# The output projection turned channel-major, with its store in 128-byte pieces and image blocks placed through DRAM

## The chip, the cores and the metric

The kernel runs on one core of a Trainium2 chip. The metric is the device time of one execution in microseconds (us), as a median over runs. The engines are TensorE (PE in the profile; its weight loads are PEld), VectorE (DVE), ScalarE (ACT), GpSimd (POOL) and SyncE (SP; here it only issues DMAs, and its queue appears as SPq).

## The reference, cut to what matters

```python
# attention with keys and values pooled 4x4 from an image, then a gated feed-forward
kv_pool = kv.reshape(B, H // r, r, W // r, r, C).mean(axis=(2, 4))     # r = 4
k = v = kv_pool.reshape(B, -1, C) @ w_sr                               # 768 keys per image
x = softmax((q @ k.T) / sqrt(C)) @ v                                   # 4 x 12288 tokens, C = 128
out = (np.maximum(x @ w_gate, 0.0) * (x @ w_val)) @ w_out              # d_ff = 1536
```

The kernel cuts the 49,152 tokens into 96 tiles of 512 (T) and the hidden layer into 12 blocks of 128 (NFB). Four tiles are a group (GRP); there are 24 groups.

## The kernel before

All stages are spread over one software pipeline: in iteration k, tile k is scored, tile k-1 takes its values, tile k-3 goes through the gated layer, and tile k-4 through the output projection. Each iteration has 12 steps, one per hidden block. The output projection uses the hidden block as the stationary operand, so four products of 128 columns are needed for 512 tokens, and the result has tokens on the partitions, ready to be stored in 2 KB rows:

```python
    def out_add(k, fb, s, o_ps, first):
        nc.tensor.matmul(
            o_ps, hTs[k][:, fb, s * 128 : (s + 1) * 128], wo16[:, fb, :],
            start=first, stop=(fb == NFB - 1), skip_group_check=True,
        )

    def out_proj(k, fb):
        if fb == 0:
            o_banks[k] = bank([128, NS, 128])
        for s in range(NS):
            out_add(k, fb, s, o_banks[k][:, s, :], fb == 0 and s == 0)

    def out_scale(k, engine, own, o_ps=None):
        if k not in o_sbs:
            o_sbs[k] = work.tile([128, NS, 128], FP32, tag="o_sb", bufs=3, name="o_sb")
        o_sb, o_ps = o_sbs[k][:, own], o_ps if o_ps is not None else o_banks[k]
        if engine is nc.scalar:
            nc.scalar.mul(o_sb, o_ps, 1.0 / X_SCALE**2)
        else:
            nc.vector.tensor_scalar(o_sb, o_ps, 1.0 / X_SCALE**2, None, op0=ALU.mult)

    def out_store(k, own):
        nc.sync.dma_start(
            out[k // GRP * GRP * T : (k // GRP + 1) * GRP * T, :].rearrange(
                "(p i s) c -> i p s c", p=128, i=GRP
            )[k % GRP][:, own], o_sbs[k][:, own],
        )
        if own.stop == NS:
            for tiles in (hTs, o_banks, o_sbs):
                del tiles[k]
```

Image blocks for the next image are turned while this one is computed: VectorE transposes within 32 by 32 blocks, and sixteen small DMAs put the blocks in their places (the iterations with this work are called image stages below, the others plain stages):

```python
    def turn_blocks(b, pair):

        blocks = work.tile([128, 2, C], FP32, tag="kv_blocks", bufs=2)
        nc.vector.transpose(
            blocks.rearrange("p h c -> p (h c)"), s3s.pop((b, pair)).rearrange("p h c -> p (h c)")
        )
        kv_Ts[b, pair] = work.tile([128, 2, 128], FP32, tag="kvT", bufs=2, name="kvT")
        return [(kv_Ts[b, pair], blocks, i, j) for i in range(4) for j in range(4)]

    def block_move(kvT, blocks, i, j):
        rows, columns = slice(32 * i, 32 * (i + 1)), slice(32 * j, 32 * (j + 1))
        nc.sync.dma_start(kvT[columns, :, rows], blocks[rows, :, columns])
...
                    if not odd and 2 <= step < 10:      # in the main loop
                        for _ in range(2):
                            block_move(*moves.pop())
```

The transposed x, on which the gated layer waits, comes from a DMA transpose in the same queue of SyncE, issued at the last step of an iteration (`x_turn(k - 1)`).

The softmax here doesn't subtract the row's maximum and nothing guards it: scores larger than these inputs give would overflow.

## Time and profile before

| | before |
|---|---|
| median time, 3 runs | 1043.85 us (1042.52 to 1044.16) |
| TensorE busy | 99% of the span |
| time of one tile in the steady part | 10.52 us |
| VectorE, ScalarE busy within such a tile | 9.36 and 9.39 us |
| DMA engines, mean share | about 36% |

A high busy share of TensorE does not show what a product costs, because matmul records overlap. The distance from one start to the next does. A line of the groups view gives line, engine, operation, output and input tiles, shape and count; then busy us and mean ns of one; then the idle time just before and what ended it. A transfer's landing is its completion, counted from its issue. Here is one stretch of SyncE's queue in an image stage, from the timeline of the kernel before (start in us, length in us, line, operation, tiles, count):

```profile
212.04 11.41 SPq L202 DMA_DIRECT2D kvT<-blocks  x16
223.55 0.53 SPq L307 DMA_DIRECT2D out_dram<-o_sb  x1
224.19 1.27 SPq L251 DMA_TRANSPOSE xT<-x  x1
```

The sixteen block moves hold this in-order queue for 11.41 us, longer than a tile, and the x transpose stands behind them. At this place TensorE did not wait, at three others it did.

### The profile page before, as it was taken

The numbers are of one execution on the slowest core, as the hardware profiler recorded it, in microseconds if no ns is written. First come the engines' busy times: TensorE is split into PE (matmuls) and PEld (weight loads), VectorE is DVE, ScalarE is ACT, GpSimd is POOL, SyncE is SP. The second block draws the span as 40 slices with busy tenths as digits, with TensorE's granted clock in tenths as the row PEclk, the third lists the DMA queues.
The fourth block names the chain that finished last, engine by engine and source line by source line (L and its number), as shares of the span: only waits on it lengthen the run. The fifth ranks groups of instructions, "written<-read, shape, count | busy, mean of one in ns | idle before, by whom it ended". The sixth has DMA issues, their size and how long they took to land.

```text
span 1041.0 us, 26051 instructions
## 1 busy us (share of the span) xinstructions
PE 1032.3 (99%) x9924; PEld 684.2 (66%) x9924; DVE 911.7 (88%) x1668; ACT 909.8 (87%) x1750; POOL 106.6 (10%) x128
## 2 busy tenths in 40 slices
PE   8999999999999999999999999999999999999998
PEld 5666666666666666666666666666666666666665
DVE  3889888898888888988888888989888888888898
ACT  4988888888888888888888888888888888888887
POOL 2000045100000015400000003440000000000000
PEclk9999999999999999999999999999999999999999
DMA  8734254441322345533223134561431322212111
GB/s 304 136 65 87 91 164 128 95 88 41 87 61 58 72 132 148 145 71 82 65 52 88 31 88 133 158 151 42 91 82 37 78 62 52 67 31 67 32 47 47
DMA packets 140253, 92.53 MB, mean 89 GB/s; under 512 B 117728, under 2 KB 118624, under 8 KB 140128
## 3 DMA queue, kind: packets, MB, share of 16 engines
q1 hardware_dynamic: 134544, 77.56, 27.7%
q0 software_dynamic: 5440, 13.24, 7.7%
q8 instruction: 77, 1.26, 0.5%
q14 instruction: 48, 0.39, 0.1%
q10 hardware_dynamic: 144, 0.07, 0.0%
HBM read 52.76 MB, written 25.17 MB: 75 GB/s over the span
## 4 chain that ended last, share of the span: by engine, by line
PE 96%; DMA 3%; SPq 0%; ACT 0%; issue 0%; DVE 0%
PE bank_ps L286 25%; PE bank_ps L265 24%; PE bank_ps L276 24%; PE bank_ps L227 12%; PE bank_ps L216 11%; DMA parts<-in_kv_dram 1%; DMA q<-in_q_dram 1%; DMA xT<-x 1%; PE bank_ps L180 0%; SPq L131 0%; ACT aT L217 0%; PE bank_ps L154 0%; PE bank_ps L172 0%; SPq L93 0%; PE bank_ps L258 0%
## 5 line engine op out<-in xcount | busy, mean ns | idle before, releaser
L279 DVE SCALAR_TENSOR_TENSOR hT<-bank_ps,val 128x512 f16<-128x512 f32 x1152 | 760.6, 687 | 99.3 <-ACT val L269 74.2
L269 ACT CAST val<-bank_ps 128x512 f16<-128x512 f32 x1152 | 678.5, 591 | 111.5 <-PE bank_ps L265 109.8
L286 PEld LDWEIGHTS <-hT 128*128 128x128 f16 x4608 | 353.1, 98 | 203.6 <-issue 0.2
L286 PE MATMUL bank_ps<-wo,hT 128*128 128x128 f16 x4608 | 443.6, 219 | 0.0
L265 PE MATMUL bank_ps<-xT,wv 128*128 128x512 f16 x1152 | 436.6, 379 | 0.4 <-DMA xT<-x 0.2
L276 PE MATMUL bank_ps<-xT,wg 128*128 128x512 f16 x1152 | 436.6, 379 | 0.0
L217 ACT ACTIVATE aT<-bank_ps 128x512 f16<-128x512 f32 x576 | 346.2, 605 | 0.9 <-PE bank_ps L216 0.8
L227 PE MATMUL bank_ps<-kv,aT 128*128 128x129 f16 x2304 | 223.5, 220 | 0.5 <-DVE kv L189 0.4
L227 PEld LDWEIGHTS <-aT 128*128 128x128 f16 x2304 | 177.2, 98 | 68.3 <-issue 0.9
L216 PE MATMUL bank_ps<-qT,kv 128*128 128x512 f16 x576 | 216.8, 379 | 0.4 <-DVE qT L114 0.2
L276 PEld LDWEIGHTS <-wg 128*128 128x128 f16 x1152 | 112.7, 98 | 65.8 <-issue 0.2
L265 PEld LDWEIGHTS <-wv 128*128 128x128 f16 x1152 | 112.7, 98 | 1.4 <-DMA xT<-x 0.9
L243 DVE TENSOR_TENSOR x<-bank_ps,rinv 128x256 f16<-128x256 f32 x188 | 79.7, 425 | 6.7
L78 POOL DMA_DIRECT2D q<-in_q_dram x23 | 12.5, 544 | 550.2 <-DMA qT<-q 549.8
L304 DVE TENSOR_SCALAR o_sb<-bank_ps 128x512 f32<-128x512 f32 (+1 forms) x95 | 64.0, 674 | 1.3 <-PE bank_ps L286 1.3
L140 POOL TENSOR_TENSOR s<-parts 128x512 f32<-128x512 f32 x36 | 45.3, 1270 | 164.1 <-DMA parts<-in_kv_dram 161.2
L216 PEld LDWEIGHTS <-kv 128*128 128x128 f16 x576 | 56.1, 98 | 2.9 <-ACT kv L174 0.8
L235 DVE RECIPROCAL rinv<-bank_ps 128x2 f32<-128x2 f32 x192 | 30.7, 160 | 0.6 <-PE bank_ps L227 0.6
L142 POOL TENSOR_TENSOR s<-s 128x512 f32<-128x512 f32 x18 | 22.8, 1268 | 1.4
L144 POOL TENSOR_TENSOR c<-s 128x256 f32<-128x256 f32 x18 | 13.1, 727 | 1.4
L165 ACT COPY kvT<-bank_ps 128x128 f32<-128x128 f32 x4 | 1.1, 266 | 10.4 <-PE bank_ps L154 9.5
L167 DVE COPY kvT<-bank_ps 128x128 f32<-128x128 f32 x2 | 0.6, 292 | 10.0 <-PE bank_ps L154 10.0
(48 smaller groups left out, 78.3 us busy)
## 6 DMA issues: line engine op xcount, KB each, us to landing
parts<-in_kv_dram SPq DMA_DIRECT2D x48, 512.0 KB, 6.2
out_dram<-o_sb SPq DMA_DIRECT2D x95, 256.0 KB, 2.1
q<-in_q_dram POOLq DMA_DIRECT2D x23, 512.0 KB, 5.4
kvT<-blocks SPq DMA_DIRECT2D x144, 8.0 KB, 1.8
xT<-x SPq DMA_TRANSPOSE x94, 2.5
q<-in_q_dram SPq DMA_DIRECT2D x2, 512.0 KB, 7.9
wv<-in_moe_w_val_dram POOLq DMA_DIRECT2D x2, 192.0 KB, 4.4
wg<-in_moe_w_gate_dram POOLq DMA_DIRECT2D x2, 192.0 KB, 5.2
```

The source lines that it names most:

```text
L140: eng.tensor_tensor(s2[:, i], parts[:, 2 * i, h], parts[:, 2 * i + 1, h], op=ALU.add)
L216: nc.tensor.matmul(s_ps, kv16[:, k // NST, jc, 0:C], qT_of(k), start=True, stop=True)
L217: nc.scalar.activation(aTs[k][:, jc, :], s_ps, AF.Exp, scale=qk_scale)
L227: nc.tensor.matmul(x_ps[:, i, :], aTs[k][:, jc, s * 128 : (s + 1) * 128], kv16[:, k // NST, jc, C : 2 * C + 1], start=(jc == 0 and i == 0) ...
L235: nc.vector.reciprocal(rinvs[k, half], x_banks[k, half][:, :, C : C + 1])
L243: nc.vector.tensor_tensor(x16s[k][:, 2 * half : 2 * half + 2, :], x_ps[:, :, 0:C], rinv.to_broadcast([128, 2, C]), op=ALU.mult,)
L265: nc.tensor.matmul(va_ps, wv16[:, fb * 128 : (fb + 1) * 128], xTs[k], start=True, stop=True)
L269: nc.scalar.copy(val, va_ps)
L276: nc.tensor.matmul(g_ps, wg16[:, fb * 128 : (fb + 1) * 128], xTs[k], start=True, stop=True)
L279: nc.vector.scalar_tensor_tensor(hTs[k][:, fb, :], g_ps, 0.0, vals.pop((k, fb)), op0=ALU.max, op1=ALU.mult)
L286: nc.tensor.matmul(o_ps, hTs[k][:, fb, s * 128 : (s + 1) * 128], wo16[:, fb, :], start=first, stop=(fb == NFB - 1), skip_group_check=True,)
L304: nc.vector.tensor_scalar(o_sb, o_ps, 1.0 / X_SCALE**2, None, op0=ALU.mult)
```

## The change

The intent is to relieve TensorE: with the output weights stationary and the hidden block moving, one product of 512 columns does the work of four, and three of four weight loads go. The result then has channels on the partitions, so VectorE transposes it in 32 by 32 blocks and GpSimd scales and arranges it. Only 32 channels of a token stay together, so the store is in pieces of 128 B. To let one store cover 16 tokens of a partition, the q load orders the tokens differently, in four DMAs; the first and last group keep the old order and take 16 stores per tile. The image blocks are placed by one store to DRAM and four loads. The last two tiles keep the old output path.

```diff
         q16 = work.tile([128, GRP * NS, C], FP16, tag="q16", bufs=2)
-        nc.gpsimd.dma_start(
-            q16, q[b, n0 : n0 + GRP * T, :].rearrange("(p s) c -> p s c", p=128)
-        )
+        rows = q[b, n0 : n0 + GRP * T, :]
+        if g in (0, NG - 1):
+            nc.gpsimd.dma_start(q16, rows.rearrange("(p s) c -> p s c", p=128))
+        else:
+            rows = rows.rearrange("(i t j s) c -> j t i s c", i=GRP, t=32, s=NS)
+            for j in range(4):
+                nc.gpsimd.dma_start(
+                    q16[32 * j : 32 * (j + 1)].rearrange("t (i s) c -> t i s c", i=GRP), rows[j]
+                )
         q16s[g] = q16
 
     def q_turn(g):
...
-        blocks = work.tile([128, 2, C], FP32, tag="kv_blocks", bufs=2)
+        blocks = work.tile([128, 4, 2, 32], FP32, tag="kv_blocks", bufs=2)
         nc.vector.transpose(
-            blocks.rearrange("p h c -> p (h c)"), s3s.pop((b, pair)).rearrange("p h c -> p (h c)")
-        )
-        kv_Ts[b, pair] = work.tile([128, 2, 128], FP32, tag="kvT", bufs=2, name="kvT")
-        return [(kv_Ts[b, pair], blocks, i, j) for i in range(4) for j in range(4)]
-
-    def block_move(kvT, blocks, i, j):
-        rows, columns = slice(32 * i, 32 * (i + 1)), slice(32 * j, 32 * (j + 1))
-        nc.sync.dma_start(kvT[columns, :, rows], blocks[rows, :, columns])
+            blocks.rearrange("p j h c -> p (j h c)"),
+            s3s.pop((b, pair)).rearrange("p j h c -> p (j h c)"),
+        )
+        placed = dram.tile([128, 256], FP32, tag="blocks", bufs=2)
+        nc.sync.dma_start(placed, blocks.rearrange("p j h c -> p (j h c)"))
+        kvT = work.tile([128, 4, 2, 32], FP32, tag="kvT", bufs=2, name="kvT")
+        kv_Ts[b, pair] = kvT
+        rows = placed.rearrange("(i p) (j x) -> j p i x", p=32, j=4)
+        return [
+            (kvT[32 * j : 32 * (j + 1)].rearrange("p i h c -> p i (h c)"), rows[j])
+            for j in range(4)
+        ]
 
     def turn_values_dma(b, pair):
         for jc in (2 * pair, 2 * pair + 1):
...
     def out_proj(k, fb):
+        if k == NT - 2:
+            if fb == 0:
+                o_banks[k] = bank([128, NS, 128])
+            for s in range(NS):
+                out_add(k, fb, s, o_banks[k][:, s, :], fb == 0 and s == 0)
+            return
         if fb == 0:
-            o_banks[k] = bank([128, NS, 128])
-        for s in range(NS):
-            out_add(k, fb, s, o_banks[k][:, s, :], fb == 0 and s == 0)
+            o_banks[k] = bank([128, T])
+        nc.tensor.matmul(
+            o_banks[k], wo16[:, fb, :], hTs[k][:, fb, :], start=fb == 0, stop=fb == NFB - 1
+        )
+
+    def out_turn(k):
+
+
+        o_t = work.tile([128, T], FP32, tag="o_t", bufs=2)
+        nc.vector.transpose(o_t, o_banks.pop(k))
+        o_sb = work.tile([128, 4, NS, 32], FP32, tag="o_sb", bufs=3)
+        nc.gpsimd.tensor_scalar(
+            o_sb.rearrange("t j s c -> t s j c"),
+            o_t.rearrange("t (s j c) -> t s j c", s=NS, j=4),
+            1.0 / X_SCALE**2, None, op0=ALU.mult,
+        )
+        del hTs[k]
+        g = k // GRP
+        rows = out[g * GRP * T : (g + 1) * GRP * T, :]
+        moves = []
+        for b in range(4):
+            o_b = o_sb[32 * b : 32 * (b + 1)]
+            if g in (0, NG - 1):
+                to = rows.rearrange("(j t i s) (b c) -> b i j t s c", j=4, t=32, s=NS, c=32)
+                moves += [(to[b, k % GRP, j], o_b[:, j]) for j in range(4)]
+            else:
+                to = rows.rearrange("(i t r) (b c) -> b i t r c", t=32, r=16, c=32)
+                moves.append((to[b, k % GRP], o_b.rearrange("t j s c -> t (j s) c")))
+        return moves
 
...
                 if step == NFB - 1 and k < last:
-                    out_scale(kO, nc.vector if kF < NT - 2 else nc.scalar, slice(0, NS))
-                    out_store(kO, slice(0, NS))
+                    out_moves = out_turn(kO)
+            if 2 <= step < 10:
+                for _ in range(2):
+                    if out_moves:
+                        nc.sync.dma_start(*out_moves.pop())
...
-                    if not odd and 2 <= step < 10:
-                        for _ in range(2):
-                            block_move(*moves.pop())
+                    if moves and step > 4:
+                        nc.sync.dma_start(*moves.pop())
```

Left out are the layout of the pooled sums (four column blocks outermost, so that a block's pieces are contiguous), the matching layout in `project`, and one buffer fewer for a pooling intermediate.

More of the change, by code (lines that the diff above doesn't have):

```diff
@@ L64 @@
     work = ctx.enter_context(tc.tile_pool(name="work", bufs=2))
+    dram = ctx.enter_context(tc.tile_pool(name="dram", bufs=1, space=bass.MemoryType.DRAM))
     psum = ctx.enter_context(tc.tile_pool(name="psum", bufs=8, space=bass.MemoryType.PSUM))
@@ L137, in pool_pixels @@
         parts = kv_in[b, pair]
-        s2 = work.tile([128, 2, r, C], FP32, tag="kv_s2", bufs=3)
+        s2 = work.tile([128, 2, r, C], FP32, tag="kv_s2", bufs=2)
         for i in range(2):
@@ L145, in pool_pixels @@
         if h == 0:
-            s3s[b, pair] = work.tile([128, 2, C], FP32, tag="kv_s3", bufs=2, name="kv_s3")
-        eng.tensor_tensor(s3s[b, pair][:, h], c2[:, 0], c2[:, 1], op=ALU.add)
+            s3s[b, pair] = work.tile([128, 4, 2, 32], FP32, tag="kv_s3", bufs=2, name="kv_s3")
+        c4 = c2.rearrange("p i (j c) -> p i j c", c=32)
+        eng.tensor_tensor(s3s[b, pair][:, :, h], c4[:, 0], c4[:, 1], op=ALU.add)
     def turn_add(chunk, lines, first=False):
@@ L178, in project @@
     def project(b, pair):
-        pr = bank([128, 2, 128])
+        pr = bank([128, 4, 2, 32])
         nc.tensor.matmul(pr, w_sr_f32, kv_Ts.pop((b, pair)), start=True, stop=True)
         nc.vector.tensor_scalar(
-            kv16[:, b, 2 * pair : 2 * pair + 2, 0:C], pr, 1.0 / (r * r), None, op0=ALU.mult
+            kv16[:, b, 2 * pair : 2 * pair + 2, 0:C].rearrange("c h (i p) -> c h i p", p=32),
+            pr.rearrange("c i h p -> c h i p"), 1.0 / (r * r), None, op0=ALU.mult,
         )
@@ L377, in add_lines @@
     def add_lines(pair):
-        s2 = work.tile([128, 2, r, C], FP32, tag="kv_s2", bufs=3, name="kv_s2")
+        s2 = work.tile([128, 2, r, C], FP32, tag="kv_s2", bufs=2, name="kv_s2")
         nc.vector.tensor_tensor(s2, line(pair, 0), line(pair, 1), op=ALU.add)
@@ L468 @@
     ready = {}
+    out_moves, moves = [], []
     last = NT + LAG - 1
```

## The prediction

> **What bounds the kernel now.** I read the page first (busy shares, then the chain that ended last), then the groups by line, then a timeline of TensorE in the steady part, then the queue of SyncE, because the change moves work onto it.
>
> ```profile
> span 1041.0 us, 26051 instructions
> ...
> PE 1032.3 (99%) x9924; PEld 684.2 (66%) x9924; DVE 911.7 (88%) x1668; ACT 909.8 (87%) x1750; POOL 106.6 (10%) x128
> ...
> PE 96%; DMA 3%; SPq 0%; ACT 0%; issue 0%; DVE 0%
> PE bank_ps L286 25%; PE bank_ps L265 24%; PE bank_ps L276 24%; PE bank_ps L227 12%; PE bank_ps L216 11%; DMA parts<-in_kv_dram 1%; DMA q<-in_q_dram 1%; DMA xT<-x 1%; PE bank_ps L180 0%; SPq L131 0%; ACT aT L217 0%; PE bank_ps L154 0%; PE bank_ps L172 0%; SPq L93 0%; PE bank_ps L258 0%
> ```
>
> TensorE is the bound nearly everywhere: 96% of the chain is matmuls, a quarter of it the output projection (L286). A busy PE says little by itself, so I looked at the spacing of its starts. In the timeline the columns are start and length in us.
>
> ```profile
> 503.15 0.39 PE L286 MATMUL bank_ps<-wo,hT 128*128 128x128 f16 x4
> 503.37 0.38 PE L265 MATMUL bank_ps<-xT,wv 128*128 128x512 f16 x1
> 503.58 0.38 PE L216 MATMUL bank_ps<-qT,kv 128*128 128x512 f16 x1
> 503.80 0.38 PE L276 MATMUL bank_ps<-xT,wg 128*128 128x512 f16 x1
> 504.02 0.39 PE L286 MATMUL bank_ps<-wo,hT 128*128 128x128 f16 x4
> 504.24 0.38 PE L265 MATMUL bank_ps<-xT,wv 128*128 128x512 f16 x1
> ```
>
> Each product of 512 columns holds the array for about 0.216 us (215.9 ns as the mean of start to start over the steady part), and four products of 128 columns for about 0.224 us (55.9 ns each). The 379 and 219 ns in the groups are latencies that overlap. There are no gaps, so TensorE's issue is saturated; one tile of 512 tokens takes 10.52 us.
>
> ```profile
> L286 PEld LDWEIGHTS <-hT 128*128 128x128 f16 x4608 | 353.1, 98 | 203.6 <-issue 0.2
> L286 PE MATMUL bank_ps<-wo,hT 128*128 128x128 f16 x4608 | 443.6, 219 | 0.0
> ...
> L304 DVE TENSOR_SCALAR o_sb<-bank_ps 128x512 f32<-128x512 f32 (+1 forms) x95 | 64.0, 674 | 1.3 <-PE bank_ps L286 1.3
> ```
>
> The 353 us of weight loads of L286 look like the prize, but the matmuls behind them have 0.0 idle before them: the loads lie entirely beside the matmuls. Removing them is worth only what the spacing of starts shows.
>
> **What the Trainium skill says.** (1) "TensorE: Matmul & The Clock Gate", section "Wait — 56ns, not 53.3ns?", gives a warm spacing of N/2.4 GHz plus a fixed cost of about 2.5 ns for each matmul, 55.6 ns at N=128 and 215.7 at N=512. The trace agrees: 55.9 and 215.9. (2) "Vector Engine (DVE) Microarchitecture Reference", section 3.8, says that the 32x32 transpose sustains one element per cycle per lane. The trace has it as 435 ns for 256 fp32 columns from SBUF; the plain scaling of 256 columns from PSUM (L304) took 425, so they are alike; nothing here shows a transpose out of PSUM. (3) "DMA: Bandwidth & Descriptors", section "Specifications", sets 512 B as the least size for line rate and says that below it SDMA does read-modify-write. The trace has 128 B packets only within SBUF (12.5 ns each, against 88 ns for a 2048 B store packet); no run yet shows 128 B packets into HBM. (4) "GPSIMD Engine Reference", section 4.1, says one-input operations run roughly at line rate there. The trace has only two-input ones of size, 1270 ns for 512 columns.
>
> **The change part by part.** *Output projection on TensorE.* 94 of 96 tiles (all but the last two) get 12 products of 512 columns in place of 48 of 128. Per hidden block: 4 x 55.9 = 223.5 ns becomes 215.9, so 7.6 ns. 94 x 12 x 7.6 ns = **8.6 us removed**, all on the bounding path. Of this 8.4 us comes before the last two iterations.
>
> *VectorE.* The scaling of a tile (681 ns) becomes a transpose of 512 columns. From 435 ns at 256 and one further column per cycle, I estimate about 700 ns. VectorE is busy 9.36 of the 10.52 us of a tile (window view), so 20 ns more is nothing; it stays under the new tile time of 10.52 - 0.09 = 10.43 us. ScalarE has 9.39 and is untouched.
>
> *GpSimd.* One scaling of 128x512 per tile. Bounded above by the two-input 1.27 us, x94 = at most 120 us, beside 107 us now: some 20% of the span, not a bound. The q load becomes four issues of about 0.53 us (now one); a key/value tile has 4.2 to 5 us of pooling. All that, with the 4.3 us wait for a q transpose, is about 12 us in the worst tile, which two buffers of the transposed tile absorb. VectorE's own L279 took 687 ns without GpSimd at work and 688 beside it, so I expect no contention.
>
> *DMA engines.* 94 x 2048 = 192,512 packets of 128 B replace 94 x 128 of 2048 B. At 12.5 ns (their SBUF rate) on 16 engines: 150 us, or 14% of the span, against 94 x 128 x 88 ns / 16 = 66 us (6%) now. Total from 36% to about 45%. At twice the packet time it would be near 60%. Both are hidden.
>
> *SyncE's queue.* This is the part that I think matters at the end.
>
> ```profile
> L202 SPq DMA_DIRECT2D kvT<-blocks x144: 585/595/1876, 169.4 to 729.6; - x144
> ```
> ```profile
> L307 SPq DMA_DIRECT2D out_dram<-o_sb x97: 333/338/1187, 49.2 to 1037.8; - x97
> ```
>
> (min/median/max issue time in ns.) The plain two-level store costs 338 ns to issue; the three-level block move 595, and a burst of them starts every 0.64 us. The key/value load, also three-level with larger rows, has the same 595, so I take levels, not descriptors, as the cost. The new stores have three levels. In the middle: 4 x 0.64 = 2.6 us per tile, where 10.43 are there; the block moves fall from 16 to 5 per pair of chunks. Harmless. But in the first and last group each tile has 16 stores: 16 x 0.64 = 10.2 us. In the first group, with 1.2 us for the x transpose and 2 us for a q transpose once, SyncE falls about 1 us per tile behind, some 5 us at most; the x transpose is needed one tile (10.4 us) after its issue and lands in 2.5, so it has 7.9 us of slack: no stall expected. In the last group the tiles 92 and 93 carry 32 such stores, while the last two iterations have no attention and last only 7.9 us each. On the old clock: tile 92's scaling begins at 1019.05, the last x transpose is issued until 1021.5, then 32 x 0.64 = 20.5 us run to 1042.0, and three plain stores stand behind them in the queue, the last at about 1042.9. Now it is issued at 1037.8. So **about 5.1 us is added at the end**.
>
> Sum: 1043.85 - 8.4 + 5.1 = 1040.5 us.
>
> **The rivals.** *A: TensorE's gain survives whole.* If a 128 B-row store issues in 0.4 us, 32 take 12.8 us, the tail is hidden, and the time is 1043.85 - 8.6 = 1035. For it: the 338 ns of the present store. Against: every three-level pattern here shows 534 or more. *B: SyncE or DMA becomes the bound.* If a store of 512 rows costs its queue far more than one of 64, say 2.4 us, then four and a transpose are 10.8 us per tile, above 10.43; with other traffic that is 1075 or more. Likewise if a 128 B write into HBM holds an engine for some 60 ns: 128 per engine and tile are 7.7 us, atop the present third, nearly full. Against: a transpose of 2048 rows holds the queue only 0.76 us longer than one of 512 (1970 against 1206), 0.5 ns per row; and SBUF packets of 128 B take 12.5 ns. For: read-modify-write below 512 B, and nothing measured to HBM. *C: SyncE's first-group delay reaches TensorE.* At 0.8 us per store the x transposes slip by 3 to 4 us per tile and use up the slack; a few us there and 10 at the end: 1046 to 1052. *D: the transpose out of PSUM runs at half rate*, about 1.2 us: VectorE at 9.9 of 10.43 us, some bank waits, about 1045.
>
> **Range and chances.** The gain can't exceed 8.6 us or 0.8% by the spacing of starts; a gain over 2% would need a TensorE saving that the trace doesn't have. The tail adds 0 to 10 us for issue times of 0.4 to 0.8 us: 1035 to 1046. B and D widen the upper side. I take 1034 to 1049. Faster by over 2% (below 1023): 0.02. Slower by over 2% (above 1064.7), mostly B: 0.09. Within: 0.89.
>
> **What would show it.** In the new profile: L286's successor with about 1128 matmuls of 512 columns spaced 0.216 us; PEld's busy share down strongly (its 3384 loads fewer) with a gain of only 0.8%; a tile time of 10.43 us; the vector transpose at about 700 ns; the new stores at about 600 ns of queue each; DMA share at 45 to 60%; TensorE ending about 8 us earlier, but the chain ending in SyncE's queue and output stores for some 5 us more than now. Wrong would be: TensorE waiting on x transposes or banks in the middle, a DMA share near full, store issues over 1 us, or a chain that ends in the last tile's own store as now.

## The result and the profile after

The changed kernel took 1035.72 us (median of 4 runs, 1035.43 to 1037.13), the kernel before 1043.71 us (4 runs). The ratio is 0.9928 with a 95% interval of 0.9911 to 0.9945: within 2%, and clearly below 1. Ratios are the mean time of one kernel's fast runs over that of the other's of the same rounds, so they are not quite the ratio of the quoted medians.

The page of the changed kernel answers the lines of the prediction as follows (busy shares, DMA queues with packets, MB and share of the 16 engines, the chain by engine, and groups):

```profile
span 1034.1 us, 19981 instructions
...
PE 1023.5 (99%) x6540; PEld 543.3 (53%) x6540; DVE 910.6 (88%) x1669; ACT 909.6 (88%) x1749; POOL 281.4 (27%) x288
...
q1 hardware_dynamic: 315648, 78.76, 39.1%
q0 software_dynamic: 14944, 13.24, 10.6%
...
PE 97%; DMA 2%; DVE 0%; SPq 0%; ACT 0%; issue 0%
...
L313 PE MATMUL bank_ps<-hT,wo 128*128 128x512 f16 x1128 | 427.5, 379 | 0.0
...
L323 POOL TENSOR_SCALAR o_sb<-o_t 128x512 f32<-128x512 f32 x94 | 140.0, 1489 | 700.8 <-DVE rinv L248 673.3
...
L313 PEld LDWEIGHTS <-wo 128*128 128x128 f16 x1128 | 110.4, 98 | 67.2
...
L321 DVE STREAM_TRANSPOSE o_t<-bank_ps 128x512 f32<-128x512 f32 x94 | 66.4, 706 | 0.0
```

TensorE is still 99% busy and still nearly the whole chain. The weight loads of the output projection fell from 353 us busy to 110 us, and all weight loads from 684 to 543 us, while the span fell by 6.9 us: nearly all of the load time that went had been hidden. The vector transpose takes 706 ns where the scaling took 681. GpSimd's scaling is the slowest new piece at 1489 ns, and GpSimd goes from 10 to 27% busy without a compute engine waiting for it. DMA traffic rises to about 50% of the engines' time (39.1 + 10.6 and small change).

The timeline of TensorE in the steady part answers the one shown before:

```profile
503.59 0.38 PE L289 MATMUL bank_ps<-xT,wg 128*128 128x512 f16 x1
503.80 0.38 PE L313 MATMUL bank_ps<-hT,wo 128*128 128x512 f16 x1
504.02 0.38 PE L278 MATMUL bank_ps<-xT,wv 128*128 128x512 f16 x1
```

Every product of 512 columns starts 0.216 us after the last, the output product (L313) among them.

To see where the 6.9 us between the two profiled spans lie, I cut each trace at the starts of the products of the value half (the first matmul of a step for x): the first such start, every twelfth (one tile) and the last.

| stage | before, us | changed, us | difference |
|---|---|---|---|
| start to first value product | 30.07 | 30.92 | +0.85 |
| the first two tiles | 17.91 | 17.82 | -0.09 |
| tiles 2 to 92 | 961.76 | 952.64 | -9.12 |
| the last tiles, to the last value product | 24.29 | 24.11 | -0.18 |
| last value product to the end | 6.98 | 8.59 | +1.61 |
| span | 1041.0 | 1034.1 | -6.9 |

The first row is not an effect that I can pin on the change: the start-up differs by about a microsecond between profiles of kernels that have it in common (29.79 us in one experiment below and 30.48 in another look at the same changed kernel). The ordinary tile falls from 10.515 to 10.425 us. In the middle stage 91 tiles x 0.09 us are 8.2 us; nearly all the rest is three tiles in image stages, 0.97 us too long together, that took 11.29, 11.25 and 11.28 us before, where their neighbours with the same extra work took 10.95. In the list of waits of the kernel before they show as waits for the transposed x:

```profile
PEld L265 <- DMA xT<-x: 0.9, 3, 0.3
```

(us in total, times, longest.) The first of the three places, from SyncE's timeline in the kernel before:

```profile
166.11 3.19 SPq L131 DMA_DIRECT2D parts<-in_kv_dram  x4
169.40 12.78 SPq L202 DMA_DIRECT2D kvT<-blocks  x16
182.29 0.53 SPq L307 DMA_DIRECT2D out_dram<-o_sb  x1
182.92 1.27 SPq L251 DMA_TRANSPOSE xT<-x  x1
```

The transposed x landed at 185.39, and the value product that needed it started at 185.44. Only once per image do four image loads stand before sixteen moves, which fits three late tiles rather than nine; SyncE's own list of waits has six waits of the moves for these loads, 5.3 us in all. In the changed kernel's list no wait for a transposed x is left, and all nine image tiles with a projection take 10.86 us.

The end is the other side of the account. SyncE's queue in the kernel before:

```profile
1019.76 0.34 SPq L307 DMA_DIRECT2D out_dram<-o_sb  x1
1020.34 1.20 SPq L251 DMA_TRANSPOSE xT<-x  x1
1027.03 11.14 SPq L307 DMA_DIRECT2D out_dram<-o_sb  x4
```

and in the changed kernel:

```profile
1011.91 1.21 SPq L264 DMA_TRANSPOSE xT<-x  x1
1013.22 16.17 SPq L535 DMA_DIRECT2D out_dram<-o_sb  x32
1029.49 1.35 SPq L352 DMA_DIRECT2D out_dram<-o_sb  x3
```

The first has four stores with long pauses between them (the 11.14 us reach from the first issue to the end of the last). The second is nearly solid: 32 small stores in 16.17 us, and then three plain stores back to back. A small store takes 0.43 us to issue and the next starts 0.474 us after it (medians); the 16.17 us also hold a pause of 0.4 us, until GpSimd has scaled tile 93, and one store of 1.07 us. The last store of all is issued 4.95 us after the last value product, against 3.82 before, 1.13 us later. Not all of that is the queue. In the kernel before, ScalarE scaled tile 93; now VectorE transposes it, falls behind, and TensorE waits for it once:

```profile
PE bank_ps L299 <- DVE hT L292: 0.2, 1, 0.2
```

So VectorE's last scaling ends 3.99 us after the last value product, against 3.75. That is 0.24 of the 1.13 us, and the queue costs the other 0.9. The execution then ends 3.64 us after the last issue, against 3.17: another 0.47 us. This landing varies: it took 2.8 to 3.2 us in the four profiles whose last tiles go the old way, 3.4 in stores_2k below, and 3.3 to 3.8 in the six with small stores there. Together the three parts are the 1.6 us of the table.

### The profile page after: what moved, and what is told of

It reads as the page before. It is cut to its first block, busy times and chain, and to the rows that moved or that the text cites. A ratio compares the mean times of both kernels' runs of the same rounds, so it can differ in the third digit from the quotient of the medians.

```text
span 1034.1 us, 19981 instructions
## 1 busy us (share of the span) xinstructions
PE 1023.5 (99%) x6540; PEld 543.3 (53%) x6540; DVE 910.6 (88%) x1669; ACT 909.6 (88%) x1749; POOL 281.4 (27%) x288
## 3 DMA queue, kind: packets, MB, share of 16 engines
q1 hardware_dynamic: 315648, 78.76, 39.1%
q0 software_dynamic: 14944, 13.24, 10.6%
## 4 chain that ended last, share of the span: by engine, by line
PE 97%; DMA 2%; DVE 0%; SPq 0%; ACT 0%; issue 0%
PE bank_ps L278 24%; PE bank_ps L289 24%; PE bank_ps L313 24%; PE bank_ps L240 12%; PE bank_ps L229 12%; DMA parts<-in_kv_dram 1%; DMA q<-in_q_dram 1%; PE bank_ps L299 0%; PE bank_ps L188 0%; DVE hT L292 0%; SPq L138 0%; ACT aT L230 0%; PE bank_ps L162 0%; PE bank_ps L180 0%; SPq L100 0%
## 5 line engine op out<-in xcount | busy, mean ns | idle before, releaser
L313 PE MATMUL bank_ps<-hT,wo 128*128 128x512 f16 x1128 | 427.5, 379 | 0.0
L323 POOL TENSOR_SCALAR o_sb<-o_t 128x512 f32<-128x512 f32 x94 | 140.0, 1489 | 700.8 <-DVE rinv L248 673.3
L313 PEld LDWEIGHTS <-wo 128*128 128x128 f16 x1128 | 110.4, 98 | 67.2
L321 DVE STREAM_TRANSPOSE o_t<-bank_ps 128x512 f32<-128x512 f32 x94 | 66.4, 706 | 0.0
L85 POOL DMA_DIRECT2D q<-in_q_dram x88 | 48.4, 557 | 0.3 <-issue 0.3
L248 DVE RECIPROCAL rinv<-bank_ps 128x2 f32<-128x2 f32 x192 | 28.0, 146 | 0.6 <-PE bank_ps L240 0.6
```

The costliest lines, as they stand in the source:

```text
L85: nc.gpsimd.dma_start(q16[32 * j : 32 * (j + 1)].rearrange("t (i s) c -> t i s c", i=GRP), rows[j])
L313: nc.tensor.matmul(o_banks[k], wo16[:, fb, :], hTs[k][:, fb, :], start=fb == 0, stop=fb == NFB - 1)
L321: nc.vector.transpose(o_t, o_banks.pop(k))
L323: nc.gpsimd.tensor_scalar(o_sb.rearrange("t j s c -> t s j c"), o_t.rearrange("t (s j c) -> t s j c", s=NS, j=4), 1.0 / X_SCALE**2, None, ...
```

## The experiments

The theory to test: the gain is (a) a fixed cost of some 2.5 ns per matmul, three times 1128 of them, 8.5 us in all, and (b) three waits for x transposes that sixteen block moves had caused, about 1 us; (c) the last group's stores, and VectorE's transpose of tile 93, give 1.6 us back; (d) the small packets cost nothing in the middle. The measured change fits: 1043.71 - 8.5 - 1.0 + 1.6 = 1035.8, against 1035.72. That it fits so closely is partly luck, since the start-up alone differs by up to 1.1 us between profiles. The main rivals were that the gain comes from which operand is stationary, and that small packets or DMA load cost something everywhere.

### narrow4: four products again, same operands

```diff
-        nc.tensor.matmul(
-            o_banks[k], wo16[:, fb, :], hTs[k][:, fb, :], start=fb == 0, stop=fb == NFB - 1
-        )
+        for s in range(4):
+            own = slice(s * (T // 4), (s + 1) * (T // 4))
+            nc.tensor.matmul(
+                o_banks[k][:, own], wo16[:, fb, :], hTs[k][:, fb, own],
+                start=fb == 0 and s == 0, stop=fb == NFB - 1, skip_group_check=True,
+            )
```

> The changed kernel, its 512-column output product cut into four of 128 columns with the same stationary wo block, everything else as changed; the result stays right. My theory (the gain in the middle is only the fixed cost of a matmul, about 2.5 ns each, 3 x 1128 more of them): the tile time goes from 10.43 back to 10.52 us and the whole to about 1035.7 + 8.6 = 1044.3 us; weight loads rise by 3384 and stay beside the matmuls. Rival (the gain came from which operand is stationary, or from having fewer weight loads of the fresh hT): the cut costs less than 3 us, about 1036 to 1038.

Measured: correct, 1043.70 us (4 runs, 1043.35 to 1044.27); ratio to the kernel before, of 1043.23 us on the same chip, 1.0003 (0.9989 to 1.0018). The tile is back at 10.515 us. The page's groups of this kernel:

```profile
L315 PEld LDWEIGHTS <-wo 128*128 128x128 f16 x4512 | 346.7, 98 | 200.3 <-issue 0.2
L315 PE MATMUL bank_ps<-hT,wo 128*128 128x128 f16 x4512 | 436.0, 219 | 0.0
```

With the weights stationary but the products narrow, the whole gain is gone. The rival that the roles of the operands matter falls: what counts is the number of products. Each product here brings its own weight load, and the loads came back with the products (x4512), so this run and the next do not separate a fixed cost of a product from one of its load; no run did.

### narrow2: two products

The edit is the same with 2 in place of 4.

> The same with two products of 256 columns. Theory of a fixed cost per matmul: 1128 more matmuls x 2.5 ns = 2.9 us, so about 1038.6 us and a tile time of 10.46 us. Rival (the weight load of 98 ns hides fully behind 256 columns and only 128-column products suffer): no cost, 1035.7 us.

Measured: correct, 1038.33 us (4 runs, 1037.51 to 1039.26); ratio 0.9952 (0.9937 to 0.9967). The tile takes 10.455 us, 0.03 us above the changed kernel's, for 12 more products: 2.5 ns each. The cost goes by the count of products (each with its load), also where a weight load of 98 ns has a product of more than 100 ns to hide behind. This settles (a): 0.09 us per tile for 36 products fewer is again 2.5 ns each.

### tail_plain: the last group's wide tiles stored in the old way

```diff
-        if k == NT - 2:
+        if k >= NT - 4:
...
-                    out_moves = out_turn(kO)
+                    if kO >= NT - 4:
+                        out_scale(kO, nc.vector if kF < NT - 2 else nc.scalar, slice(0, NS))
+                        out_store(kO, slice(0, NS))
+                    else:
+                        out_moves = out_turn(kO)
```

> The changed kernel with the tiles 92 and 93 projected and stored in the old way, so that the 32 small stores before the end are gone. Theory (these stores hold the queue of SyncE past the end of the work, and cost about 1.1 us of issue, 0.5 us of landing, and 0.2 us of TensorE waiting on VectorE; the last value product to the end took 8.6 us against 7.0 before): about 1.8 us less, and 0.18 us more for 24 wider products lost, so about 1034.1 us. Rival (the tail is set by the last tile's own work, the stores are hidden): 1035.9 us, slightly more than the changed kernel.

Measured: correct, 1034.25 us (4 runs, 1034.11 to 1034.63); ratio 0.9913 (0.9898 to 0.9928). From the last value product to the end it took 6.85 us. One image tile took 11.58 us in this profile, 0.72 above the rest; another look below did not have it. So the new way of the last two wide tiles was what lengthened the end. This edit takes away both the run of small stores and VectorE's transpose of tile 93 (its last scaling ends 3.75 us after the last value product again); the next experiment tells them apart. This kernel also beats both others, so it was run again beside the changed kernel (after_again and tail_plain_again).

### stores_2k: stores of the old shape, to wrong places

```diff
-        rows = out[g * GRP * T : (g + 1) * GRP * T, :]
-        moves = []
-        ...
-        return moves
+        to = out[g * GRP * T : (g + 1) * GRP * T, :].rearrange("(p i s) c -> p i (s c)", p=128, i=GRP)
+        return [(to[:, k % GRP], o_sb.rearrange("t j s c -> t (j s c)"))]
```

> The changed kernel with one store per tile in 2 KB rows, to wrong places on purpose (the result is wrong). Theory (the 128-byte pieces are hidden everywhere but at the end): the middle tiles stay at 10.43 us, and only the tail shortens by about 1.5 us: 1034.2 us. Rival (small HBM packets slow the other transfers and so TensorE or the first tiles): a gain of over 3 us and fewer waits in the middle.

Measured: 1034.60 us (4 runs, 1034.16 to 1035.17), wrong result as intended; ratio 0.9918 (0.9901 to 0.9934). The tiles of the middle are what they were to the last digit, 10.425 us, with 952.64 us for tiles 2 to 92 in both. From the last value product to the end it took 7.43 us, so the end shortened by 1.16 us, less than the 1.5 that I had expected; the last store was issued 4.05 us after the last value product, not 3.82. The 0.23 us that stay are VectorE's transpose of tile 93, which this edit keeps (its last scaling still ends 3.99 us after). So the small stores held the queue back by 0.90 us, 4.95 less 4.05. The DMA queue of this kernel

```profile
q1 hardware_dynamic: 129504, 78.74, 30.1%
```

has 186,144 packets fewer and nine points less of the engines' time, and TensorE does not notice. This settles (d): at 50% the DMA engines hide the 128 B pieces in the middle.

### blocks_only: the image blocks alone

The kernel before takes over only the hunks on the pooled sums, `project`, `turn_blocks` and the loads in the main loop (the last two are printed in the change above):

```diff
-                    if not odd and 2 <= step < 10:
-                        for _ in range(2):
-                            block_move(*moves.pop())
+                    if moves and step > 4:
+                        nc.sync.dma_start(*moves.pop())
```

> The kernel before with only the placing of the image blocks through DRAM taken over (one store and four loads per pair in place of sixteen moves); the output projection and stores as before. Theory (in the kernel before, three tiles of the image stages are 0.34 us longer than their neighbours, where TensorE waits 0.9 us in all for a transposed x held up behind the sixteen moves in the queue of SyncE; in the changed kernel these waits are gone): 0.9 to 1.0 us less than before, about 1042.8 us, and no wait for x transposes at those three places. Rival (the waits went away only with the changed output path): no difference, the three waits are still there.

Measured: correct, 1041.85 us (5 runs, 1040.77 to 1042.03) against 1042.56 us of the kernel before; ratio 0.9989 (0.9976 to 1.0003), so by time alone a gain of 1 us is likely but not proven. The trace is clear: the three long tiles are gone (all nine image tiles at 10.95 us), and the list of waits has none for x transposes. In the timeline the stretch of the queue shown before has become

```profile
209.89 0.33 SPq L202 DMA_DIRECT2D placed<-blocks  x1
210.27 2.40 SPq L213 DMA_TRANSPOSE kv<-kv  x2
212.78 2.09 SPq L542 DMA_DIRECT2D kvT<-placed  x4
```

The placing takes 2.4 us of the queue in place of 11.4. Since the output path is untouched here, (b) belongs to this part of the change alone.

### stores_16: small stores for every tile

```diff
-                to = rows.rearrange("(i t r) (b c) -> b i t r c", t=32, r=16, c=32)
-                moves.append((to[b, k % GRP], o_b.rearrange("t j s c -> t (j s) c")))
+                to = rows.rearrange("(i t j s) (b c) -> b i j t s c", t=32, j=4, s=NS, c=32)
+                moves += [(to[b, k % GRP, j], o_b[:, j]) for j in range(4)]
```

> The changed kernel with sixteen small stores for every tile, as the first and last group have them, in place of four. Theory (the queue of SyncE is the resource nearest to its limit): 16 x 0.475 = 7.6 us, 1.3 us for an x transpose and about 1 us per tile for q transposes are 9.9 us of the 10.43 us, so plain stages still hide it; in the image stages another 3 us per tile make it 13 us, the queue falls behind by some 3 us per tile for 8 to 10 tiles, eats the 7.9 us of slack of the x transpose, and TensorE waits: 10 to 60 us in all, 1045 to 1095 us. Rival (the DMA engines, not the queue, are what could have been a limit; bytes and packets are the same): 1036 us as before.

Measured: correct, 1121.48 us (4 runs, 1120.79 to 1122.62); ratio 1.0756 (1.0742 to 1.0771): 79 us slower than the kernel before and 86 us over the changed kernel, more than the 60 us that I had as the upper end. From the list of waits of this kernel (the first two lines are largely the same waits, of the weight load and of its product), and one stretch of SyncE's timeline in an image stage:

```profile
PEld L278 <- DMA xT<-x: 50.4, 30, 6.4
PE bank_ps L278 <- DMA xT<-x: 36.9, 21, 5.9
PE bank_ps L188 <- DMA kvT<-placed: 23.7, 9, 3.7
```

```profile
153.86 1.20 SPq L264 DMA_TRANSPOSE xT<-x  x1
155.42 2.68 SPq L138 DMA_DIRECT2D parts<-in_kv_dram  x4
158.20 12.05 SPq L535 DMA_DIRECT2D out_dram<-o_sb  x16
170.36 1.22 SPq L264 DMA_TRANSPOSE xT<-x  x1
```

The two x transposes, one per tile, are 16.5 us apart where a tile has 10.43: the four image loads and the sixteen stores lie between them. The stores took 0.43 us each here too, but the run has two pauses, of 1.9 and 2.6 us, before the seventh and the eighth store. SyncE's own waits name what they waited for:

```profile
SPq L535 <- DMA parts<-in_kv_dram: 27.1, 18, 2.6
```

The semaphores recorded with the trace go round by eight in this queue: each DMA waits until the one eight places before it has landed. The seventh store so waited for the third image load, the eighth for the fourth. The expectation had added up issue times alone and left these waits out.

TensorE stood still for 60.6 us by the two PE lines: for transposed x, and for the image blocks, whose loads from DRAM stand behind the stores as well. The rest of the 86 us came with a lower clock: the granted clock was 0.98 over the whole of all four executions, against 1.0 in the changed kernel, and 0.51 from 170.8 to 177.7 us, a stretch that takes in the end of the longest wait; TensorE was busy 24.6 us longer for the same matmuls.

The tiles of the image stages took mostly 11 to 16.5 us. In the plain stages between them most tiles stayed at 10.43 us, as expected. The DMA engines' throughput was not the limit: the hardware queue's share was 35.7% here, below the changed kernel's 39.1%, for the same bytes. So what overran is SyncE's in-order queue, by its issue times and by its waits for earlier DMAs to land. Four stores per tile in the middle are what keeps the change clear of it; the different q order, which looks like a detail of the diff, buys that.

### after_again and tail_plain_again: the two best on one chip

> The changed kernel once more, beside the next one on the same chip. 1035.7 us if nothing has moved; last value product to the end about 8.6 us in its profile.

> The changed kernel with tiles 92 and 93 in the old way, once more, now on the same chip as the changed one. Theory (the queue of SyncE is late at the end by about 1.1 us and the landing behind small stores by 0.5 us): 1.3 to 1.8 us less than the changed kernel. Rival (the difference of the first try was that of the chips): the same time.

Measured: the changed kernel 1035.96 us (5 runs, 1035.27 to 1036.08), ratio 0.9930; the changed kernel with the plain tail 1034.35 us (4 runs, 1033.76 to 1034.81), ratio 0.9915. The ranges do not meet, and the difference of medians is 1.6 us, near the 1.61 us of the table of stages less the 0.18 us that two tiles without wide products give up. In the look at the plain tail the queue has pauses again between its last four stores:

```profile
1017.75 11.13 SPq L352 DMA_DIRECT2D out_dram<-o_sb  x4
```

With stores_2k this settles (c), and this kernel is the fastest. The looks at the changed kernel also differ a little in the middle: in after_again one image tile took 11.15 us, 0.29 above the rest, so a wait there can still occur now and then. Its x transpose took 7.8 us to land, against 2.4 at the median.

### stores_8: what sets the issue time

```diff
-                to = rows.rearrange("(i t r) (b c) -> b i t r c", t=32, r=16, c=32)
-                moves.append((to[b, k % GRP], o_b.rearrange("t j s c -> t (j s) c")))
+                to = rows.rearrange("(i t h r) (b c) -> b i h t r c", t=32, h=2, r=8, c=32)
+                moves += [
+                    (to[b, k % GRP, h], o_b[:, 2 * h : 2 * h + 2].rearrange("t j s c -> t (j s) c"))
+                    for h in range(2)
+                ]
```

> The changed kernel with eight stores per tile in the middle groups, each of 256 rows of 128 B in the form 8 x 32 elements, in place of four of 512 rows (issue 0.62 us each). It asks what sets the issue time. If the number of rows does (128 rows took 0.43, 512 took 0.62, so 0.5 ns per row, as with the transposes): about 0.49 us each. If the form does (rows of a second level within a partition cost 0.43 whatever their number): 0.43 us. If half the bytes change nothing: 0.62 us. In any case eight are at most 5 us of a tile's 10.43 us of queue in the plain stages, with an x transpose of 1.2 us; the time stays within 3 us of the changed kernel unless the image stages fill the queue.

Measured: correct, 1035.93 us (one run of unknown state, so only a sign that it is no slower). The view of the tile o_sb (min/median/max ns of issue):

```profile
L538 SPq DMA_DIRECT2D out_dram<-o_sb x800: 315/449/2989, 51.3 to 1029.0; - x160
```

The median of the 256-row form alone is 449 ns, against 430 for 128 rows and 620 for 512 rows. Twice the rows cost 19 ns, so neither the count of rows (which asked for 0.49 us) nor half the bytes (0.62) explains it; the form is nearest. The 512 rows go as one run of 512, not as 16 x 32, and that form is dearer by 170 ns. Why it is, and why the old block moves of 64 rows between two places in SBUF took 595 ns, these runs do not tell.

## Why the prediction was right or wrong

The measured 1035.72 us lies in the range (1034 to 1049) and in the class that had 0.89. The point, 1040.5, was 4.8 us too high: 3.5 us of that is the end of the kernel, and 1.0 us the block moves. By its own steps:

1. **Removed on TensorE, 8.6 us.** Right in mechanism and size: the tile fell by 0.09 us, which over 94 tiles is 8.5 us. narrow4 and narrow2 show it to be a cost per product with its load.
2. **VectorE about 700 ns for the transpose.** Right: 706 ns, and nobody waits for it in the middle. Rival D falls. The step overlooked that tile 93 had been scaled by ScalarE: there the transpose is new work for VectorE, and cost 0.24 us.
3. **GpSimd at most 1.27 us for the scaling.** Wrong as a bound: 1489 ns. The step took a two-input operation on contiguous data as an upper bound for a one-input one with a permuted output in runs of 32. It did not matter in the middle, with GpSimd at 27%; at the end SyncE's queue paused 0.4 us for it. The wait of 4.3 us for a q transpose, which the step also counted, did not arise: GpSimd, now paced by the scaling, issues its q load at its place in the program rather than one group ahead. The load now runs beside the q transpose of SyncE, whose landing went from 4.3 to 8.9 us at the median, and its hold on the queue from 2.0 to 3.9. That overlap is my reading of the issue times; no run isolates it, and it is hidden.
4. **DMA share to about 45%, up to 60% at twice the packet time.** Right for the stores: they make nine points of the 50% (stores_2k), where the step had eight. The rest, some five points, it did not count; the q load's queue alone went from 7.7 to 10.6%. A 128 B packet into HBM took 13.3 ns in the mean of the trace, against the 12.5 assumed. stores_2k shows that it is hidden; that half of rival B falls.
5. **SyncE's queue: 32 stores x 0.64 us add 5.1 us at the end.** This is the step that failed. The chain and its order were as described, but the term was mis-sized: the stores started every 0.474 us, not every 0.64, and took 16.2 us with their pauses in place of 20.5, so the last store went out 1.13 us later rather than 5.1, and 0.24 of that was VectorE's; the slower landing, which the step did not have, added 0.47. The cause is the sentence "I take levels, not descriptors, as the cost": three-level patterns (three nested strides) took 595 ns in the kernel before, but in the form of the last group 430, as the issue times of the changed kernel and of stores_8 show. (The stores of the middle took 620, so there its 0.6 us held.) The prediction had named, as a sign of being wrong, a chain that ends in the last tile's own work, and it came: the chain still ends with VectorE's last scaling. The chain follows engines, so the 0.9 us of queue behind it had to be read from the timeline. So rival A came nearest, for a reason between its own and mine: its 0.4 us is nearly the issue time that was measured, but the tail is not hidden wholly, as tail_plain shows.
6. **The block moves "from 16 to 5 per pair of chunks. Harmless."** A term was left out. They were not harmless in the kernel before: three tiles lost 0.97 us in all, and the line that shows it was in the list of waits, small enough to be passed over. blocks_only shows that it goes with the sixteen moves.
7. **First-group slip, rival C.** No wait for a transposed x came from it: the first two tiles are as long as before, less what the wider products save. stores_16 shows that the mechanism is real once the queue is overfull, and that it is the image stages where it bites.

## What to carry to other kernels

Count what a removed weight load or a wider product is worth from the distance between starts, not from busy times: here weight loads lost 141 us of busy time, and the 3384 matmuls that went with them were worth 2.5 ns each, 8.5 us. When a change turns one DMA into many, add up the issue times in the queue per tile and at the end, with a duration measured for the very form; a form that only looks alike was off by a quarter. Add what those DMAs wait for: in stores_16 the stores stood still until image loads before them had landed. An in-order queue that is too long for one tile delays whatever stands behind it, so look there for small waits that come back at regular places.

## What the Trainium skill lacked or had wrong

- "DMA: Bandwidth & Descriptors", section "Specifications", asks for 512 B for line rate and warns of read-modify-write below. The trace agrees on the rate: 13.3 ns for a 128 B packet into HBM is 9.6 bytes per ns, and 88 ns for a 2048 B packet is 23. A cost of the read-modify-write itself does not show, with 12.5 ns for 128 B within SBUF. What the page lacks is when the rate matters: replacing 186,144 small packets by large ones changed no tile time here (10.425 us both ways).
- No page read gives the issue time of a store by its form on this chip. Measured in SyncE's queue: 338 ns for 128 contiguous rows of 2 KB (524 in stores_2k, where they come right behind an x transpose), 430 ns for 4 x 32 rows of 128 B, 449 for 8 x 32, 620 for one run of 512, and 595 for 2 x 32 rows between two places in SBUF.
- "GPSIMD Engine Reference", section 4.1, has one-input operations roughly at line rate. A scaling of 128x512 fp32 that permutes runs of 32 took 1489 ns, more than a two-input addition of contiguous data of that size (1270 ns). No run has the scaling without the permutation, so for contiguous data the page is not refuted.
- "TensorE: Matmul & The Clock Gate", section "Wait — 56ns, not 53.3ns?", was borne out: its 2.5 ns per matmul is what narrow2 and narrow4 measured, for a matmul with its weight load. The page has the number; what it lacks is the sum that a reader needs, 12 x 3 x 2.5 ns = 0.09 us per tile here.
